# Two layers of attention and MLP on one core: the rows' preparation for the seven-product MLP laid out anew, and the last block's h kept on chip

## The chip, the cores and the metric

The kernel runs on one core of one Trainium2 chip, in one launch. The metric is the device time in microseconds. Three runs of the kernel before gave 3548.34, 3548.96 and 3552.73 us; their median, 3548.96, is the time before.

## The reference

Two layers, with the same weights in both: x is 2048 x 640, wqkv 640 x 1920, wo 640 x 640, w1 640 x 1536, w2 1536 x 640, all fp32, 32 heads of 20 columns.

```python
x = x + _A_ref(_layernorm(x), A_wqkv, A_wo)            # attention and its output product
x = x + _B_ref(_layernorm(x), B_w1, B_b1, B_w2, B_b2)  # the MLP
# and the same two lines once more

def _B_ref(x, w1, b1, w2, b2):
    h = jnp.einsum("bsd,df->bsf", x, w1) + b1
    r = jnp.where(h > 0, h, 0)
    h = r * r
    return jnp.einsum("bsf,fd->bsd", h, w2) + b2
```

## The kernel before

**Numbers.** Each fp32 operand is split into a high part in fp32r (a cast, on ScalarE) and a low part (the rest, a subtraction, on VectorE by split_to and into, on POOL for some). A product is the sum of three: hi x hi, hi x lo, lo x hi (THREE).

**Heads.** At the end of attention, add_heads goes over four blocks of 512 rows, 0 to 3. For each of a block's four row tiles and each half of its columns it runs a chain of matmuls (L510), adds x (L1441), and calls between: 32 such points in all. At these points the first block's rows are made ready for the MLP (BESIDE_HEADS), and pieces of w_1 of 512 KB are loaded (weights_at: 20 of 24; the other four go to steps of the first block).

**A block's rows** (class Forms): four row tiles are loaded, their means and variances taken (stats, L315 on VectorE, two small operations on POOL), normalised and turned in 32 x 32 squares (turned: L348, L353 on VectorE), written to d_t and fetched back turned (fetch). Then POOL forms sums and differences (sums, third, fourth, all L342) and each operand is split: B11, B22, T1, T2, T3, T4, the fifth part of the columns (plain) and its difference (diff, giving xd). ScalarE's part of a split is L458, VectorE's L459; T3 and T4 have their low part on POOL. B21 is split last, by late(), since it shares its tile. Tile pairs 0 and 1 (rows 0 and 2, rows 1 and 3) go one after the other, so T4(1) is the last split but one. PLACES says at which step each of these stands.

**First product** (class Up). 1536 columns of h are six units of a block. One unit is a Winograd form of a 2 x 2 product, seven products in place of eight: 54 matmuls of 128 x 256 (L1461). Their order on TensorE: A11 (6), the fourth sum S4 of the unit before (9), S2 (6), S1 (6), A22 (6, and 3 on xd), S3 (9), A12 (9). VectorE adds between PSUM banks: L1499 after S2 (S3 goes on in that bank, so it waits for it), L1507, L1508 and L1509 after S3 (L1508 frees the bank that S4 takes), L1522 in the unit's tail. ScalarE applies relu (L1488) and squares (L1511, L1524), POOL forms two sums of h (L1527, L342) for the second product, and SP stores h (d_h) and a sum (d_h1). A unit calls side() seven times, after each product; so a block has 42 steps, and at step n the next block does PLACES[n], the block after that PLACES[n - 42]. At the end of a block, late() splits B21 of the next.

**Second product** (class Down): eight pairs of row tiles (un 0 to 7), seven products too, in a group of four (grp 0, L1616) and one of three (grp 1), three pairs of h columns each. h comes back by DMA (fetch, three to five steps ahead), is split by parts (L327 on ScalarE, L328 on VectorE, after a subtraction L1595 or L1603; make, two steps ahead). The first two un are interleaved, group by group. During the last block of the first product, steps 27, 29, 33 fetch the first h, 38 and 41 make the first operands, and 15 of the 28 pieces of w_2 are loaded (bring). Instructions of one engine run in the order in which the code records them; nothing reorders them later. DMAs all go through SP's queue (L78).

In the first layer the fourth block of rows does the second product plainly (blocks = 3).

Of the kernel before, what the change touches and what calls it, by code (L numbers as in the profile page):

```python
# [8 lines left out]
F32 = mybir.dt.float32  # L9
# [28 lines left out]
LAST_PREP = 22  # L38


@with_exitstack
def tile_layers(
# [320 lines left out]
    class Forms:  # L363
# [4 lines left out]
            -4: [("stats", 0)],  # L368
            -3: [("stats", 2)],
            0: [("load", 1), ("load", 3)],  # L370
            2: [("turned", 0)],
            8: [("fetch", 0)],
            9: [("turned", 2)],
            10: [("stats", 1)],
            12: [("stats", 3)],
            15: [("fetch", 2)],
            16: [("turned", 1)],
            19: [("turned", 3)],
            22: [("fetch", 1)],
            23: [("sums", 0), ("split", B11, 0)],  # L380
            24: [("third", 0), ("split", B22, 0)],
            25: [("plain", 0)],
            26: [("split", T1_, 0), ("fetch", 3)],
            27: [("split", T2_, 0)],
            28: [("fourth", 0)],
            30: [("split", T3_, 0)],
            31: [("split", T4_, 0)],
            32: [("diff", 0), ("sums", 1), ("split", B11, 1)],
            33: [("third", 1), ("split", B22, 1)],
            34: [("plain", 1)],  # L390
            35: [("split", T1_, 1)],
            37: [("split", T2_, 1), ("fourth", 1)],
            38: [("split", T3_, 1)],
            40: [("split", T4_, 1)],
            41: [("diff", 1)],
# [889 lines left out]
    def attention(first, x_src, first_rows):  # L1285
# [27 lines left out]
        def begin(i):  # L1313

            t, u = divmod(i, NKT)
            g, qb = divmod(t, NQB)
            if u == 3:
                q_t.pop(t - 1, None)
            if u == 1:
                if t + 2 < NBLK and t + 2 not in q_t:  # L1320
                    load_q(t + 2)
            if u % 4 == 1 and qb == 0:
                k_t.pop((g - 1, u // 4), None)
                for h in (0, 1, 2, 3) if g else (1, 2):
# [12 lines left out]
            if (t, u) in loads:  # L1337
                loads[t, u]()
            if t == NBLK - 1 and u == 12:
                first_rows.extend(row_tile(x_src, i) for i in range(4))  # L1340
            if i in split:
                split.pop(i)()
# [83 lines left out]
    def add_heads(qb, x_src, x_mid, xs, side):  # L1426

        ot = ready.pop(qb)
        for i in range(4):
            if qb + 1 < NQB:  # L1430
                xs.append(row_tile(x_src, qb * 4 + 4 + i))
# [12 lines left out]

    class Up:
# [36 lines left out]
        def unit(self, qb, j, x, whole, free):  # L1482
# [5 lines left out]
            relu = lambda out, src, f: nc.scalar.activation(  # L1488
                out, src, AF.Relu, bias=b1_t[:, f : f + 1]
            )  # L1490
# [15 lines left out]
            r = slot([P, 2, 4, P], F32, "r")  # L1506
            add(u0, bank[1], u0)  # L1507
            add(r[:, 1, 1::2, :], rc(bank[2]), rc(u0))  # L1508
            add(r[:, 0, 1::2, :], rc(bank[3]), rc(u0))  # L1509
            relu(r[:, :, 1::2, :], r[:, :, 1::2, :], j + NP)  # L1510
            nc.scalar.activation(r[:, :, 1::2, :], r[:, :, 1::2, :], AF.Square)  # L1511
            side()
            self.chain(bank[0], j, A12, x, True, (0, last[:, :, 0]))
            relu(r[:, 0, 0::2, :], rc(bank[0]), j)
# [5 lines left out]
            def tail():  # L1520
                self.chain(bank[2], j, S4, x, True, (0, last[:, :, 1]))
                add(r[:, 1, 0::2, :], rc(bank[2]), rc(u1))  # L1522
                relu(r[:, 1, 0::2, :], r[:, 1, 0::2, :], j)
                nc.scalar.activation(r[:, :, 0::2, :], r[:, :, 0::2, :], AF.Square)  # L1524
                s = u0.rearrange("p (u c) -> p u c", u=2)
                if whole:
# [11 lines left out]
                self.held.append(store)  # L1538
# [4 lines left out]
    class Down:  # L1543
# [4 lines left out]
        def __init__(self, blocks, x_mid, x_dst):  # L1548
            self.x_mid, self.x_dst, self.blocks = x_mid, x_dst, blocks
            self.steps = [  # L1550
                (un, grp, j) for grp in (0, 1) for j in range(NP // 2) for un in range(2)
            ]
            self.steps += [
                (un, grp, j)
                for un in range(2, 2 * NQB)
# [3 lines left out]
            self.uses = [(n, un, j) for n, (un, grp, j) in enumerate(self.steps) if grp != 1]  # L1559
# [3 lines left out]
        def fetch(self):  # L1563
# [8 lines left out]
            if qb < self.blocks:  # L1572
                s = self.s[un, j] = xtile("s")[:, : 4 * P].rearrange("p (f i c) -> p f i c", f=2, i=2)
                dma(nc.sync, s[:, 0], d_h1[qb, 2 * j : 2 * j + 2, :, u].rearrange("i p c -> p i c"))

# [42 lines left out]
        def run(self, side):  # L1618

            last_j = NP // 2 - 1  # L1620
            for n, (un, grp, j) in enumerate(self.steps):
# [12 lines left out]
                if grp and un and j == (0 if grp == 1 and un > 1 else 1):  # L1634
# [3 lines left out]
                while self.uses and self.uses[0][0] <= n + (  # L1638
                    3 if n < NP or self.uses[0][1] == 2 * NQB - 1 and self.blocks < NQB else 5
# [95 lines left out]
    def layer(first, x_a, x_m, x_e, front_0, ahead):  # L1735
# [36 lines left out]
        def between():  # L1772
            side()
            n = beside[0]
            made[0].do(Forms.BESIDE_HEADS, n)
            made[1].do(Forms.PLACES, {29: -9, 30: -4, 31: -3}.get(n))
            more(weights_at.get(n, 0))
            beside[0] += 1

        for qb in range(NQB):  # L1780
            add_heads(qb, x_a, x_m, xs, between)
            if qb > 1:
                all_steps()
        made[0].y.clear()
# [6 lines left out]
        def bring(n):  # L1791
            for _ in range(n):
# [4 lines left out]
        lead = {27: down.fetch, 29: down.fetch, 31: lambda: down.rows(0), 33: down.fetch,  # L1797
                38: down.make, 41: down.make}
        for qb in range(NQB):
            for n in range(7 * NP):  # L1800
                def step(n=n, qb=qb):
                    if qb + 1 < NQB:
                        made[qb + 1].do(Forms.PLACES, n)
                        if qb + 2 < NQB:
                            made[qb + 2].do(Forms.PLACES, n - 7 * NP)
                        if n % 3 == 1:
                            more(1)
                    else:
                        bring(int(n % 7 in (1, 4) or n % 14 == 6))
                        lead.get(n, lambda: None)()  # L1810
                steps.append(step)
            x = made[qb].res
            for j in range(NP):
                up.unit(qb, j, x, qb < blocks, qb == NQB - 1)
            all_steps()
            made[qb].res = None
            if qb + 1 < NQB:
                del x[B21]
                made[qb + 1].late()
# [3 lines left out]
        down.rows(1)  # L1823
# [85 lines left out]
```

## Time and profile before

| what | value |
|---|---|
| median of three runs | 3548.96 us |
| the profiled execution | 3550.9 us, its span 3548.8 us |
| TensorE matmul busy | 3503.0 us, 99% of the span |
| VectorE, ScalarE, POOL busy | 2776.4, 2833.4, 965.2 us |
| mean granted clock of TensorE | 0.997 |
| first product, first layer | 1444.55 to 1623.74 us |
| first product, second layer | 3213.91 to 3389.36 us |

The span is what the profiler saw on the core; the execution's own time has some 2 us more around it. The timeline gives start, duration, engine, line, operation, tiles and the count of like instructions in a row; in brackets stands how long the engine was idle before, and what released it.

### The profile page before, as it was taken

Reading aid. Unit: us, or ns where it says so; the run is one execution under the profiler, and the core shown is the slowest. Engines: PE = TensorE matmul, PEld = TensorE weight load, DVE = VectorE, ACT = ScalarE, POOL = GpSimd, SP = SyncE. Lnnn points to the kernel's source line nnn. Section 1 sums busy time; section 2 is a strip of 40 time slices with the busy share of each in tenths; the row PEclk is TensorE's granted clock in tenths of the full one; section 3 lists DMA queues with packets and bytes.
Section 4 is the critical chain, followed back from the end, with each engine's and each line's share of the span. In section 5 each row is a group of like instructions: output and inputs, shape, how many; then the busy total and the mean of one; then the engine's idle time right before and its main releaser. Section 6 shows DMA issues by size and latency. Waiting matters only on the chain. (4 is left out here: it accounts for less than half of the span.)

```text
span 3548.8 us, 74211 instructions
## 1 busy us (share of the span) xinstructions
PE 3503.0 (99%) x26404; PEld 2161.2 (61%) x26404; DVE 2776.4 (78%) x5512; ACT 2833.4 (80%) x5026; POOL 965.2 (27%) x1189
## 2 busy tenths in 40 slices
PE   9999999999999999899999999999999999999999
PEld 8998333333333336899989973333333333368999
DVE  8999888888888882666869988888888888726567
ACT  5889999999999994354348899999999999944533
POOL 4430354444321211440143201212112121214400
PEclk9999999999999999999999999999999999999999
DMA  7765444444322137758656652222232121377584
GB/s 258 231 209 184 144 137 145 122 132 135 120 69 61 52 104 256 246 182 305 240 192 226 197 170 69 79 74 61 69 85 57 43 60 52 107 274 244 196 293 146
DMA packets 335041, 534.46 MB, mean 151 GB/s; under 512 B 75604, under 2 KB 154964, under 8 KB 334672
## 3 DMA queue, kind: packets, MB, share of 16 engines
q1 hardware_dynamic: 334144, 528.02, 46.7%
q8 instruction: 209, 3.42, 0.4%
q10 hardware_dynamic: 528, 1.70, 0.1%
q14 instruction: 160, 1.31, 0.1%
HBM read 339.01 MB, written 190.55 MB: 149 GB/s over the span
## 5 line engine op out<-in xcount | busy, mean ns | idle before, releaser
L939 ACT ACTIVATE e<-banks 128x512 f32<-128x512 f32 (+1 forms) x3416 | 2035.2, 692 | 55.9 <-PE banks L929 20.7
L846 DVE TENSOR_REDUCE mx<-banks 128x1 f32<-128x512 f32 x2560 | 1620.4, 684 | 321.4 <-PE banks L835 269.9
L944 PE MATMUL banks<-e,vg 128*32 128x512 f32 x8192 | 1093.4, 605 | 2.1 <-ACT e L939 2.0
L835 PE MATMUL banks<-k,q 60*128 60x512 f32 x3360 | 1058.7, 410 | 0.0
L929 PE MATMUL banks<-q,k 62*128 62x512 f32 x4096 | 1049.8, 441 | 1.3 <-ACT v L606 0.6
L929 PEld LDWEIGHTS banks<-q,k 62*128 62x128 f32 x4096 | 515.0, 184 | 748.7 <-ACT e L939 440.9
L835 PEld LDWEIGHTS banks<-k,q 60*128 60x128 f32 x3360 | 567.7, 185 | 195.1 <-ACT e L939 63.7
L875 DVE CUSTOM_DVE_ANT_0 rl<-banks,rl 128x512 f32<-128x512 f32 x736 | 476.9, 688 | 31.0 <-PE banks L835 6.8
L868 ACT ACTIVATE rl<-banks 128x512 f32<-128x512 f32 x736 | 399.7, 602 | 57.0 <-PE banks L835 46.4
L944 PEld LDWEIGHTS banks<-e,vg 128*32 128x32 f32 x8192 | 162.2, 108 | 352.9 <-issue 269.0
L1461 PE MATMUL banks<-xf,w 128*128 128x256 f32 x2448 | 315.3, 288 | 26.7 <-DVE r L1508 10.4
L542 PE MATMUL banks<-xnT,wqk 64*128 64x512 f32 x1080 | 326.5, 392 | 0.0
L530 PE MATMUL banks<-xnT,wqk 64*128 64x512 f32 x1080 | 325.7, 393 | 0.0
L1461 PEld LDWEIGHTS banks<-xf,w 128*128 128x128 f32 x2448 | 303.1, 194 | 36.0 <-DVE r L1508 14.2
L988 POOL TENSOR_TENSOR few<-few,minus_t 128x16 f32<-128x16 f32 x62 | 179.9, 2901 | 232.1 <-DMA few<-d_s 231.9
L339 POOL CAST mr<-nt 128x32 fp32r<-128x32 f32 x64 | 13.4, 210 | 755.6 <-DVE nt L901 755.6
L999 POOL TENSOR_TENSOR o<-o 128x512 f32<-128x512 f32 x62 | 79.5, 1283 | 502.2 <-DMA o<-d_r 276.8
L835 PE MATMUL banks<-kd,q 60*128 60x512 f32 x736 | 209.9, 398 | 0.8 <-ACT rl L868 0.6
L542 PEld LDWEIGHTS banks<-xnT,wqk 64*128 64x128 f32 x1080 | 201.2, 187 | 8.6
L530 PEld LDWEIGHTS banks<-xnT,wqk 64*128 64x128 f32 x1080 | 199.3, 186 | 9.1 <-issue 1.7
L530 PE MATMUL banks<-wv,xnT 64*128 64x320 f32 x960 | 193.5, 308 | 0.0
L542 PE MATMUL banks<-wv,xnT 64*128 64x320 f32 x960 | 190.4, 306 | 0.0
(149 smaller groups left out, 3530.8 us busy)
## 6 DMA issues: line engine op xcount, KB each, us to landing
q<-d_qk SPq DMA_DIRECT2D x876, 80.0 KB
d_qk<-ev SPq DMA_DIRECT2D x80, 512.0 KB
k<-d_qk SPq DMA_DIRECT2D x444, 80.0 KB
x<-d_x SPq DMA_DIRECT2D x96, 320.0 KB
w<-d_w SPq DMA_DIRECT2D x60, 480.0 KB
w<-d_w SPq DMA_DIRECT2D x48, 512.0 KB
d_h<-r SPq DMA_DIRECT2D x48, 512.0 KB
r<-d_h SPq DMA_DIRECT2D x48, 512.0 KB
```

Of the source, the lines that this page charges most:

```text
L530: top = nc.tensor.matmul(dst, a[:64], b[:64], start=start, stop=last)
L542: low = nc.tensor.matmul(dst, a, b, start=False, stop=last, skip_group_check=True)
L835: nc.tensor.matmul(dst, q_t[t][b : b + 60, p, sub * P : (sub + 1) * P], k_t[t // NQB, c][b : b + 60, p, :], start=True, stop=True,)
L846: nc.vector.tensor_reduce(maxima(t)[:, 2 * p + par, sub, c : c + 1], dst, axis=AX.X, op=ALU.max)
L868: nc.scalar.activation(r, dst, AF.Relu)
L875: nc.vector.tensor_tensor_reduce(out=r[par], in0=dst, in1=r[par], scale=1.0, scalar=LEAST, op0=ALU.add, op1=ALU.max, accum_out=maxima(t)[: ...
L929: nc.tensor.matmul(dst, k_t[t // NQB, kt // 4][b : b + 62, p, (kt % 4) * P : (kt % 4 + 1) * P], q_t[t][b : b + 62, p, :], start=True, stop ...
L939: nc.scalar.activation(dst, src, AF.Exp, scale=SCALE)
L944: nc.tensor.matmul(acc[32 * h : 32 * h + 32, :], v_t[t // NQB, kt // 8][:, kt % 8, 32 * h : 32 * h + 32], es[p][:, par, :], start=(kt == 0 ...
L988: nc.gpsimd.tensor_tensor(few, few, minus_t, op=ALU.pow)
L999: nc.gpsimd.tensor_mul(o[:, 0, :], o[:, 0, :], o[:, 1, :])
L1461: nc.tensor.matmul(dst, w, v, start=n == 0 and not more, stop=n == len(todo) - 1, skip_group_check=more,)
```

## The change

Line numbers from 39 on go up by two, and by 16 to 42 in Up and Down (L1499 becomes L1498, L1507 to L1509 become L1523 to L1525, L1522 becomes L1546, L1595 becomes L1637).

- The heads are added in the order of blocks 1, 0, 2, 3 (HEADS), the first product goes over the blocks 1, 2, 3, 0 (UPS); the second goes from 0 up as before. The ring of PSUM tiles is set to bank 7 ahead of the heads.
- PLACES is another table: stats, fetches, sums and splits stand at other steps. late() stands at step 2 of its own block.
- Beside the heads one piece of w_1 is loaded at every odd point below 28, 14 in all; the other ten at every third step of the first block.
- The last block, block 0, keeps its h: relu and square write to six arena tiles and POOL's sums to six other tiles, which Down's first two un read. Its 24 stores and fetches a layer fall away. Relu, square and POOL's two operations there are done for each half apart. Down's operands are first made at steps 36 and 40, its rows loaded at 30, w_2 brought 22 pieces deep, and un 0 goes through both groups before un 1.

The core of the diff (of the table one line, "..." marks what is left out):

```diff
+HEADS = (1, 0, 2, 3)
+UPS = (1, 2, 3, 0)
...
-            40: [("split", T4_, 1)],
-            41: [("diff", 1)],
+            40: [("split", T3_, 1), ("fourth", 1)],
+            41: [("split", T4_, 1), ("diff", 1)],
...
-        def unit(self, qb, j, x, whole, free):
+        def unit(self, qb, j, x, whole, free, keep=None):
...
-            r = slot([P, 2, 4, P], F32, "r")
+            if keep is None:
+                r = slot([P, 2, 4, P], F32, "r")
+                of = [r[:, u] for u in range(2)]
+                pair = [r[:, :, i::2, :] for i in range(2)]
+            else:
+                of, sums = keep
+                pair = None
...
+                elif whole:
+                    for z, s in zip(of, sums):
+                        nc.gpsimd.tensor_tensor(s, z[:, 2, :], z[:, 3, :], op=ALU.add)
+                        pool_lo(z[:, 2, :], z[:, 0, :], z[:, 2, :])
...
-                self.held.append(store)
+                if pair:
+                    self.held.append(store)
...
+        def keep(self, j):
+            i = j % 2
+            for un in range(2):
+                if i == 0:
+                    self.raw[un, j // 2] = slot([P, 2, 4, P], F32, "r")
+                    self.s[un, j // 2] = xtile("s")[:, : 4 * P].rearrange(
+                        "p (f i c) -> p f i c", f=2, i=2
+                    )
+            return (
+                [self.raw[un, j // 2][:, i] for un in range(2)],
+                [self.s[un, j // 2][:, 0, i] for un in range(2)],
+            )
...
-        weights_at = {g: 1 for g in [*range(2, 8), *range(9, 15), *range(17, 23), 25, 27]}
+        ps_all.n = 7
...
-            more(weights_at.get(n, 0))
+            made[UPS[0]].do(Forms.BESIDE_HEADS, n)
+            made[UPS[1]].do(Forms.PLACES, {29: -9, 30: -3, 31: -1}.get(n))
+            more(n % 2 if n < 28 else 0)
...
-        lead = {27: down.fetch, 29: down.fetch, 31: lambda: down.rows(0), 33: down.fetch,
-                38: down.make, 41: down.make}
+        lead = {30: lambda: down.rows(0), 36: down.make, 40: down.make}
...
+                    if n == 2 and m:
+                        made[UPS[m]].late()
+                    if final:
+                        bring(int(n < 7 or n % 7 in (1, 3, 5)))
```

How the order of instructions moves, at three places.

ScalarE at the border of the first two blocks of the first layer, from the copy of u0 in the last unit (L1494, L1493) on; xf tiles are operands of the next block, t and y what they are split from (t the sums, y the turned rows). Before:

```order
L1494 COPY us_17134<-banks 128x256
L458 CAST xf_17014<-t_17090 128x2x128
L1488 ACTIVATE r_17104<-r_17104,b_t 128x2x128
L1524 ACTIVATE r_17104<-r_17104 128x4x128
L458 CAST xf_17033<-t_17090 128x2x128
L458 CAST xf_17066<-y_16919 128x2x128
L1488 ACTIVATE r_17208<-r_17208,b_t 128x4x128
L1511 ACTIVATE r_17208<-r_17208 128x4x128
L458 CAST xf_17075<-t_17090 128x2x128
```

and now:

```order
L1493 COPY us_17129<-banks 128x256
L1515 ACTIVATE r_17101<-r_17101,b_t 128x2x128
L1521 ACTIVATE r_17101<-r_17101 128x4x128
L460 CAST xf_17012<-t_17137 128x2x128
L460 CAST xf_17027<-t_17137 128x2x128
L1527 ACTIVATE r_17198<-r_17198,b_t 128x4x128
L1521 ACTIVATE r_17198<-r_17198 128x4x128
L460 CAST xf_17066<-y_16911 128x2x128
L1515 ACTIVATE r_17198<-banks,b_t 128x2x128
L460 CAST xf_17075<-t_17137 128x2x128
```

The cast of T3 (xf_17066) stood ahead of the last unit's relu and square and now stands behind them; T4's (xf_17075) has one more operation ahead of it.

POOL at the same place, from the last sum of the unit before on; the last rows are the low parts of T3 (into xf_17066) and T4 (into xf_17075) and, between t and y, "fourth". Before:

```order
L342 TENSOR_TENSOR r_17104<-r_17104 128x2x128
L342 TENSOR_TENSOR t_17090<-y_16885,t_17090 128x256
L342 TENSOR_TENSOR xf_17066<-y_16919,xf_17066 128x2x128
L318 TENSOR_TENSOR mv_17177<-mv_17177,eps_t 128x1
L319 TENSOR_TENSOR mv_17177<-mv_17177,half_t 128x1
L318 TENSOR_TENSOR mv_17193<-mv_17193,eps_t 128x1
L319 TENSOR_TENSOR mv_17193<-mv_17193,half_t 128x1
L342 TENSOR_TENSOR xf_17075<-t_17090,xf_17075 128x2x128
```

and now:

```order
L344 TENSOR_TENSOR r_17101<-r_17101 128x2x128
L320 TENSOR_TENSOR mv_17183<-mv_17183,eps_t 128x1
L321 TENSOR_TENSOR mv_17183<-mv_17183,half_t 128x1
L344 TENSOR_TENSOR xf_17066<-y_16911,xf_17066 128x2x128
L344 TENSOR_TENSOR t_17137<-y_16871,t_17137 128x256
L344 TENSOR_TENSOR xf_17075<-t_17137,xf_17075 128x2x128
```

"fourth" came ahead of T3's low part and now stands behind it; the statistics of one row tile (mv) are gone from this stretch.

VectorE at the last unit of the last block of the first layer; hb and ha are the first operands of the second product. Before:

```order
L1499 TENSOR_TENSOR us_18712<-banks,us_18712 128x256
L1595 TENSOR_TENSOR s_18624<-s_18624,r_18622 128x256
L328 TENSOR_TENSOR hb_18748<-r_18622,hb_18748 128x512
L328 TENSOR_TENSOR ha_18751<-s_18624,ha_18751 128x512
L1507 TENSOR_TENSOR us_18712<-banks,us_18712 128x256
L1508 TENSOR_TENSOR r_18774<-banks,us_18712 128x2x128
```

and now:

```order
L1637 TENSOR_TENSOR s_18308<-s_18308,r_18307 128x256
L330 TENSOR_TENSOR hb_18745<-r_18307,hb_18745 128x512
L330 TENSOR_TENSOR ha_18748<-s_18308,ha_18748 128x512
L1498 TENSOR_TENSOR us_18718<-banks,us_18718 128x256
L1523 TENSOR_TENSOR us_18718<-banks,us_18718 128x256
L1524 TENSOR_TENSOR r_18635<-banks,us_18718 128x2x128
```

The three operations of the operands stood behind the add L1499 and now stand ahead of it.

More of the change, by code (lines that the diff above doesn't have):

```diff
@@ L1339, in begin @@
             if t == NBLK - 1 and u == 12:
[L1340 removed]
+                first_rows.extend(row_tile(x_src, 4 * HEADS[0] + i) for i in range(4))
             if i in split:
@@ L1521, in tail @@
                 self.chain(bank[2], j, S4, x, True, (0, last[:, :, 1]))
[L1522 to L1526, printed above, removed]
+                add(of[1][:, 0::2, :], rc(bank[2]), rc(u1))
+                relu(1, 0)
+                square(pair[0] if pair else of[1])
+                if whole and pair:
+                    s = u0.rearrange("p (u c) -> p u c", u=2)
                     nc.gpsimd.tensor_tensor(s, r[:, :, 2, :], r[:, :, 3, :], op=ALU.add)
                     pool_lo(r[:, :, 2, :], r[:, :, 0, :], r[:, :, 2, :])
+                elif whole:
+                    for z, s in zip(of, sums):
+                        nc.gpsimd.tensor_tensor(s, z[:, 2, :], z[:, 3, :], op=ALU.add)
+                        pool_lo(z[:, 2, :], z[:, 0, :], z[:, 2, :])
                 if free:
@@ L1796, in layer, with step @@
         up = Up(side)
-        lead = {27: down.fetch, 29: down.fetch, 31: lambda: down.rows(0), 33: down.fetch,
-                38: down.make, 41: down.make}
-        for qb in range(NQB):
+        lead = {30: lambda: down.rows(0), 36: down.make, 40: down.make}
+        for m, qb in enumerate(UPS):
+            final = m == NQB - 1
             for n in range(7 * NP):
[L1801 to L1809, printed above, removed]
-                        lead.get(n, lambda: None)()
+                def step(n=n, m=m, final=final):
+                    if n == 2 and m:
+                        made[UPS[m]].late()
+                    if final:
+                        bring(int(n < 7 or n % 7 in (1, 3, 5)))
+                        lead.get(n, lambda: None)()
+                        return
+                    made[UPS[m + 1]].do(Forms.PLACES, n)
+                    if m + 2 < NQB:
+                        made[UPS[m + 2]].do(Forms.PLACES, n - 7 * NP)
+                    if n % 3 == 1:
+                        more(1)
                 steps.append(step)
             x = made[qb].res
+            if m:
+                del made[UPS[m - 1]].res[B21]
+                made[UPS[m - 1]].res = None
             for j in range(NP):
-                up.unit(qb, j, x, qb < blocks, qb == NQB - 1)
+                up.unit(qb, j, x, final or qb < blocks, final, down.keep(j) if final else None)
             all_steps()
[L1816 to L1819, printed above, removed]
+        made[UPS[-1]].res = None
         del x
```

89 lines of the change are left out of this document (49 added, 40 removed).

## The prediction

> **What bounds the kernel now.** I read the busy times on the page first, then the waits of TensorE, then TensorE's timeline through both MLPs, and last the granted clock in the stretches where it stalls.
>
> ```profile
> PE 3503.0 (99%) x26404; PEld 2161.2 (61%) x26404; DVE 2776.4 (78%) x5512; ACT 2833.4 (80%) x5026; POOL 965.2 (27%) x1189
> ```
>
> The rows of the waits of TensorE give the line that waits, what it waits for, us in total, times, the longest:
>
> ```profile
> PE banks L1461 <- DVE r L1508: 10.4, 11, 1.6
> PE banks L1461 <- DVE us L1499: 8.9, 14, 1.4
> PE banks L1616 <- ACT hb L327: 6.9, 2, 5.2
> ```
>
> TensorE is the bound: 3503.0 of a span of 3548.8 us. The change neither adds nor drops a matmul, so it can only win back lost time, and the waits put nearly all of that on the first product (L1461) and the start of the second (L1616). The timeline of TensorE in the first layer gives places (start, us, count, idle before in brackets):
>
> ```profile
> 1444.55 0.87 PE L1461 MATMUL banks<-xf,w 128*128 128x256 f32 x6
> 1448.48 0.39 PE L1461 MATMUL banks<-xf,w 128*128 128x256 f32 x1 [3.06 <-ACT xf L458]
> 1450.53 3.99 PE L1461 MATMUL banks<-xf,w 128*128 128x256 f32 x17 [1.66 <-DVE xf L459]
> ...
> 1464.09 0.52 PE L1461 MATMUL banks<-xd,w 128*128 128x256 f32 x3
> ...
> 1477.05 0.52 PE L1461 MATMUL banks<-xd,w 128*128 128x256 f32 x3
> ...
> 1492.73 3.13 PE L1461 MATMUL banks<-xf,w 128*128 128x256 f32 x24 [0.81 <-DVE us L1499]
> 1497.48 3.72 PE L1461 MATMUL banks<-xf,w 128*128 128x256 f32 x27 [1.62 <-DVE r L1508]
> ...
> 1508.07 0.52 PE L1461 MATMUL banks<-xd,w 128*128 128x256 f32 x3
> ...
> 1514.55 0.52 PE L1461 MATMUL banks<-xd,w 128*128 128x256 f32 x3
> ```
>
> The three xd matmuls mark each unit once. An undisturbed unit lasts 1514.55 - 1508.07 = 6.48 us, 0.12 a matmul. From these rows: the start should reach its second marker after 9.36 us of matmuls (24 up to the first marker, 54 more), at 1453.91, and reaches it at 1464.09: 10.2 us lost. Four units around the border of the first two blocks take 31.02 us in place of 25.92: 5.1 lost. The second layer and the second product:
>
> ```profile
> 1636.14 0.56 PE L1616 MATMUL banks<-w,hb 128*128 128x320 f32 x2 [1.68 <-ACT hb L327]
> ...
> 3213.91 0.87 PE L1461 MATMUL banks<-xf,w 128*128 128x256 f32 x6
> 3229.29 0.52 PE L1461 MATMUL banks<-xd,w 128*128 128x256 f32 x3
> 3405.32 2.44 PE L1616 MATMUL banks<-w,hb 128*128 128x320 f32 x6 [5.23 <-ACT hb L327]
> ```
>
> The second layer loses 3229.29 - 3213.91 - 9.36 = 6.0 us at its start.
>
> ```profile
> 1373.00:1444.00 71.00, 71.00 (x483) 70.34 (x480) 31.77 (x60) 4.38 (x12) 7.42 (x14) 1.00 0.97 342
> 1450.00:1460.00 10.00, 8.48 (x38) 8.19 (x39) 7.59 (x19) 1.35 (x5) 3.77 (x8) 0.50 0.78 285
> 1495.00:1500.00 5.00, 3.38 (x29) 3.18 (x28) 2.65 (x9) 2.18 (x6) 3.47 (x8) 1.00 0.74 262
> 1636.00:1641.00 5.00, 4.33 (x17) 4.07 (x18) 2.19 (x5) 1.33 (x4) 0.00 (x0) 0.66 1.04 400
> ```
>
> The last three columns are granted clock, DMA share, GB/s. The DMA engines are full (0.97) before the first product, and the clock falls to 0.50 after the 3.06 + 1.66 us of stall and to 0.66 around 1636, but stays 1.00 through the stall of 1.62.
>
> **The change, part by part.** Sums are against the profiled execution, 3550.9 us (span 3548.8); the median of the runs is 3548.96, so a sum is moved down by 1.9 at the end.
>
> A, the start of the first product. The transfer that ends last there is the fourth transposed row tile:
>
> ```profile
> w<-d_w SPq DMA_DIRECT2D x48, 512.0 KB
> 1439.30 3.17 SPq L78 DMA_DIRECT2D y<-d_t  x4
> 1446.40 0.72 POOL L342 TENSOR_TENSOR t<-y,y 128x256 f32<-128x256 f32 x1 [7.44 <-DMA y<-d_t]
> ```
>
> It was issued from 1439.30 on, and POOL, which builds the sums from it, waited 7.44 us for it. By the table of loads, 18 pieces of w_1 were issued before that fetch and 11 are now: 7 x 0.524 MB at the 342 GB/s of the window above are 10.7 us of DMA time that no longer stand ahead. That is as much as the whole lost 10.2, so what remains is set by the next thing. PSUM tiles for the heads now begin one bank later (n=7), so that the first unit's A11 takes a bank that the last head has just filled; it waits for the last add of the heads, which on VectorE stands behind stats of the next block, whose rows are loaded only two adds before. I have no row of that wait: it is at least one stats (a BN_STATS pair near 0.9, below) and at most some 4.5 us, an estimate: a load that is issued two adds earlier and takes as long as POOL waited here, 7.44, less the 3 us or so that two column halves of the heads last. Nearer the lower, since the queue is shorter: 1.3. A gives 10.2 - 1.3 = 8.9 and 6.0 - 1.3 = 4.7: -13.6 (between -8 and -15).
>
> B, the start of the second product. The 144 matmuls of its first two column pairs should need 144 x 1.76/12 = 21.1 us. The rows, of the last unit and of the second product in both layers:
>
> ```profile
> 1618.80 0.42 DVE L1499 TENSOR_TENSOR us<-banks,us 128x256 f32<-128x256 f32 x1 [0.35 <-PE banks L1461]
> 1620.34 3.56 PE L1461 MATMUL banks<-xf,w 128*128 128x256 f32 x27
> 1620.80 0.68 DVE L328 TENSOR_TENSOR ha<-s,ha 128x512 fp32r<-128x512 f32 x1
> 1623.74 1.04 PE L1616 MATMUL banks<-w,hb 128*128 128x320 f32 x6
> 1649.85 1.04 PE L1616 MATMUL banks<-w,hc 128*128 128x320 f32 x6
> 3386.13 1.22 DVE L328 TENSOR_TENSOR ha<-s,ha 128x512 fp32r<-128x512 f32 x1
> 3389.36 1.04 PE L1616 MATMUL banks<-w,hb 128*128 128x320 f32 x6
> 3392.01 1.92 PE L1616 MATMUL banks<-w,hb 128*128 128x320 f32 x12
> 3393.77 1.92 PE L1616 MATMUL banks<-w,ha 128*128 128x320 f32 x12
> 3418.16 1.04 PE L1616 MATMUL banks<-w,hc 128*128 128x320 f32 x6
> ```
>
> 1.76 is 3393.77 - 3392.01. In the second layer 3418.16 - 3389.36 = 28.8, 7.7 too many, of which 5.23 are the wait for an h read back. In the first layer 1649.85 - 1623.74 = 26.1, 5.0 too many, with 1.68 in one wait and half clock behind it. With h kept on chip neither wait exists: -5.0 and -7.7, and the second layer's last unit no longer loses the 0.5 or so that a split's 1.22 (the row of 3386.13) is over the 0.68 of the first layer's. What is late next: the first h operands are made at step 36, not 38, and on VectorE their lo parts now stand ahead of L1498 (before: L1499) of the last unit. The last of them ended at 1620.80 + 0.68 = 1621.48; with 0.42 for the add the third sum can begin at 1621.9, where it began at 1620.34: 1.6 us, and up to 2.0 with the 1.22 that this line takes in the second layer, each 1.8. B: -5.0 - 8.2 + 3.6 = -9.6 (between -5 and -12). The 24 DMAs fewer in each layer, and w_2 brought 22 pieces deep rather than 15, lie on queues that nobody there waits for once h is kept; the 24 more, shorter POOL adds are behind the same unit's relu and hold nobody.
>
> C, the borders of blocks, three in each layer. Rows of the last unit of the first block:
>
> ```profile
> 1493.88 0.77 DVE L459 TENSOR_TENSOR xf<-t,xf 128x256 fp32r<-128x256 f32 x1 [1.21 <-ACT xf L458]
> 1494.57 0.87 DVE L315 BATCH_NORM_STATS2 bst<-x 128x6 f32<-128x320 f32 x2
> 1497.34 0.41 DVE L1509 TENSOR_TENSOR r<-banks,us 128x256 f32<-128x256 f32 x1
> 1498.55 0.63 ACT L1511 ACTIVATE r<-r 128x512 f32<-128x512 f32 x1
> 1499.08 0.39 ACT L458 CAST xf<-t 128x256 fp32r<-128x256 f32 x1
> 1499.55 0.73 POOL L342 TENSOR_TENSOR xf<-t,xf 128x256 fp32r<-128x256 f32 x1 [1.37 <-ACT xf L458]
> ```
>
> Before, the split of T4 was the one thing left behind this unit's square: hi at 1499.08, lo on POOL until 1500.28, just when the next block's A22 (21 matmuls after 1497.48, 1500.0) wants it. Now T3's hi is behind the square too, and on POOL T3's lo, then "fourth", then after another cast T4's lo. From 1499.08: 0.39 + 0.08 to POOL, 0.73 (T3 lo), 0.75 (fourth, an operation of the same size), 0.45 (T4 hi), 0.75 (T4 lo): 1502.2, so A22 stalls by 2.1 where it stalled 0.2. Behind it on VectorE: the lo of xd, one stats, the tail add and the first add of the new block stand in that order, so the third sum waits 0.5; B21's split, moved from the border to step 2, ends after A12 wants it, 0.4; and B21's lo and the turned tile together put the fourth sum back by 0.9. Against that, stats of the second row tile no longer stand ahead of L1508 (0.87 + 0.2, for one more lo of some 0.6: 0.45 off the 1.62) and T1's lo no longer ahead of L1499 (0.3 off the 0.81). Net 1.9 + 0.5 + 0.4 + 0.9 - 0.75 = +2.95 at each of the first two borders. At the third no stats and no turned tile are in the way: +2.0. Twice 7.9: +15.8 (between 0, if T3 and T4 hide, and +20).
>
> D, the clock. A stall of 2.1 lies between 1.62, after which the clock held, and 1.68 + 0.53 (the two waits around 1636, as the timeline has them), after which it fell. If it falls, some 3.3 us of work run at half rate and cost 1.7. Six borders, a chance of a third: +3.
>
> The Trainium skill ("TensorE: Matmul & The Clock Gate", Part 1: The HAM clock gate) says that the array halves its clock after an idle window of some 3.4 us, windows that run freely. By that a stall of 2.1 would never be a whole idle window and D would be 0; the rows above, with a halved clock behind stalls of 2.2 spread over a window, speak for a lower point.
>
> Sum: -13.6 - 9.6 + 15.8 + 3 = -4.4, 3546.5 for a profiled execution, **3544.6** as a median.
>
> **The rivals.** R1, the borders cost nothing. If POOL takes T3 and "fourth" earlier than I think, or TensorE reaches A22 later because S4 waits on VectorE anyway, C and D are 0 and A and B stand: -23.2, 3525.8. For it: 1.62 us of stall ahead of the same matmuls give slack. Against: that stall and the square end on the same add (1497.34), so the chain keeps its length from there. R2, the clock falls at each border and stays down for two windows, as it did for the 10 us of 1450 to 1460 behind two stalls. Each border then costs 2 x 1.7; six are 20 in place of 3: -4.4 + 17 = +12.6, 3561.6. It decides where stalls within one window pass 2.2, that is, where the A22 stall of 2.1 and the 0.5 at the third sum, 1.1 us of matmuls later, fall into one window. For it: the closeness of 2.1 to 2.2. Against: the clock was 1.00 over the present border. By the skill's rule of a whole idle window R2 could not happen. R3, the kept h brings nothing, because the operands' splits on ScalarE and VectorE are as late as the fetch was: B is 0, -4.4 + 9.6 = +5.2, 3554.2. Against: ACT waits for DMA at L327 here, and the added stall is a VectorE one.
>
> **How the numbers follow.** No change, to what this measurement can tell, is within 0.2%, 7.1 us. The forecast has 0.52, its own range 3535 to 3553 from the bounds of A, B and C together; it crosses -7.1 in a third of that: 0.16 faster, 0.34 the same, 0.02 slower. R1 0.26, all faster. R2 0.17, of it 0.15 slower, 0.02 the same. R3 0.05, the same by 0.04, slower by 0.01. Faster 0.42, the same 0.40, slower 0.18. The range reaches to R1 and R2 and leaves about 0.1 beyond each: 3525 to 3561.
>
> **What would show it.** A: the second xd marker at about 11 us after the first matmul (now 19.5 and 15.4), granted clock 1.00 there. B: no wait of L1616 for a DMA behind hb, one wait of 1.6 to 2.0 on VectorE's us at the last unit. C: at each border one wait of about 2 us for the lo on POOL, and 0.4 to 0.9 behind it; the stall of 1.62 smaller. D: the clock over each border. I am wrong if the borders have no new wait (then R1), if the clock is near 0.5 over the new block's first unit (R2), or if the start still waits for the transposed tile.

## The result and the profile after

The changed kernel takes 3569.40 us (median of four runs, 3566.06 to 3571.27) against 3549.54 before (four runs): a ratio of 1.0054, with an interval of 1.0036 to 1.0071. It is slower by 20 us, where 3544.6 was forecast and 3561 was the end of the range.

The busy times of the profiled execution (3570.83 us, span 3569.1), and the waits of TensorE that belong to the MLP:

```profile
PE 3511.4 (98%) x26404; PEld 2167.9 (61%) x26404; DVE 2787.7 (78%) x5512; ACT 2837.6 (80%) x5038; POOL 973.1 (27%) x1213
```

```profile
PE banks L1463 <- DVE r L1524: 16.3, 14, 3.9
PE banks L1463 <- issue: 8.9, 2, 5.0
PE banks L1463 <- DVE us L1498: 8.5, 11, 1.6
PE banks L1463 <- ACT xf L460: 7.1, 6, 1.2
PE banks L1463 <- DVE xf L461: 2.9, 5, 1.0
PE banks L1463 <- POOL xf L344: 2.5, 6, 0.4
```

The matmuls are as many as before, but take 8.4 us more, and the mean granted clock is 0.994 in place of 0.997: more of them ran at half clock. The wait of the second product on a fetched h (6.9 before) is gone from the list. In its place stand two waits of "issue", six on a cast and six on POOL, and L1524 (L1508 before) went from 10.4 to 16.3. TensorE's timeline in the first layer says where:

```profile
1449.18 4.61 PE L1463 MATMUL banks<-xf,w 128*128 128x256 f32 x24 [5.05 <-issue]
...
1460.11 0.52 PE L1463 MATMUL banks<-xd,w 128*128 128x256 f32 x3
...
1478.88 4.99 PE L1463 MATMUL banks<-xf,w 128*128 128x256 f32 x27 [2.42 <-DVE r L1524]
...
1491.79 3.14 PE L1463 MATMUL banks<-xf,w 128*128 128x256 f32 x24 [1.07 <-DVE us L1498]
1496.42 2.78 PE L1463 MATMUL banks<-xf,w 128*128 128x256 f32 x21 [1.49 <-DVE r L1524]
1500.39 0.38 PE L1463 MATMUL banks<-xf,w 128*128 128x256 f32 x1 [1.20 <-ACT xf L460]
1501.20 0.86 PE L1463 MATMUL banks<-xf,w 128*128 128x256 f32 x5 [0.42 <-POOL xf L344]
1501.90 0.52 PE L1463 MATMUL banks<-xd,w 128*128 128x256 f32 x3
1503.01 1.86 PE L1463 MATMUL banks<-xf,w 128*128 128x256 f32 x10 [0.59 <-DVE us L1498]
1505.83 1.94 PE L1463 MATMUL banks<-xf,w 128*128 128x256 f32 x14 [0.97 <-DVE xf L461]
1508.33 3.50 PE L1463 MATMUL banks<-xf,w 128*128 128x256 f32 x27 [0.56 <-DVE r L1524]
...
1632.76 3.65 PE L1463 MATMUL banks<-xf,w 128*128 128x256 f32 x27 [1.64 <-DVE us L1498]
1636.25 1.04 PE L1658 MATMUL banks<-w,hb 128*128 128x320 f32 x6
...
1646.81 1.04 PE L1658 MATMUL banks<-w,hc 128*128 128x320 f32 x6
```

From top to bottom: 5.05 us before the first matmul of the first product; 2.42 in the fourth unit of the first block, where nothing stood before; in the block's last unit 1.07 and 1.49, where 0.81 and 1.62 stood before; at the border behind them the waits at A22 (1.20 and 0.42), S3 (0.59), A12 (0.97) and S4 (0.56), one behind the other; 1.64 at the last unit; and a second product that starts without a gap (72 matmuls in 10.56 us, 0.147 each).

To compare kernels I add up three losses in each profile, both layers together. *Start*: from the end of the heads to the second group of xd matmuls, less 9.36. *Blocks*: what the intervals between the 23 later groups have over 6.48 each. *Last*: from the last such group to the second product, less 3.6. Half clock is in these sums.

| kernel | start | blocks | last | median, us | ratio to before (interval) |
|---|---|---|---|---|---|
| before | 15.9 | 26.6 | 0.8 | 3549.54 | |
| changed | 12.0 | 58.3 | 4.1 | 3569.40 | 1.0054 (1.0036 to 1.0071) |
| bank | 13.6 | 54.1 | 4.1 | 3569.55 | 1.0049 (1.0034 to 1.0064) |
| bank, stats later | 10.0 | 55.2 | 4.1 | 3566.86 | 1.0042 (1.0028 to 1.0056) |
| w_1 as before | 24.7 | 48.8 | 4.1 | 3572.15 | 1.0056 (1.0041 to 1.0071) |
| fetches as before | 12.6 | 49.3 | 4.1 | 3563.32 | 1.0033 (1.0022 to 1.0044) |
| T3, fourth earlier | 15.7 | 45.9 | 4.1 | 3558.07 | 1.0017 (1.0007 to 1.0027) |
| table of before | 12.5 | 27.2 | 4.1 | 3539.43 | 0.9965 (0.9952 to 0.9978) |
| that, B21 at step 2 | 13.3 | 34.5 | 4.1 | 3547.72 | 0.9989 (0.9980 to 0.9999) |
| first mended kernel | 1.5 | 32.4 | 0.4 | 3530.73 | 0.9941 (0.9926 to 0.9956) |
| second mended kernel | 2.2 | 27.2 | 0.4 | 3524.93 | 0.9922 (0.9905 to 0.9938) |

The runs of before that stand beside the experiments have medians of 3551 to 3552 us, so the ratios are what to compare between rows. The losses are those of one execution each: the start differs by up to 4 us (12.0 to 15.7) between kernels that do the same there.

### The profile page after: what moved, and what is told of

It reads as the page before. It is cut to its first block, busy times and chain, and to the rows that moved or that the text cites. A ratio compares the mean times of both kernels' runs of the same rounds, so it can differ in the third digit from the quotient of the medians.

```text
span 3569.1 us, 74141 instructions
## 1 busy us (share of the span) xinstructions
PE 3511.4 (98%) x26404; PEld 2167.9 (61%) x26404; DVE 2787.7 (78%) x5512; ACT 2837.6 (80%) x5038; POOL 973.1 (27%) x1213
## 4 chain that ended last, share of the span: by engine, by line
PE 88%; DMA 4%; DVE 2%; issue 2%; ACT 2%; POOL 1%; SPq 1%; DVEq 0%; POOLq 0%; ACTq 0%
PE banks L946 27%; PE banks L931 18%; PE banks L837 17%; PE banks L1658 8%; PE banks L532 5%; PE banks L544 5%; PE banks L1463 4%; PE banks L512 2%; DMA y<-d_t 1%; SPq L80 1%; DVE xf L461 1%; DMA x<-d_x 1%; PE banks L527 1%; DMA d_t<-x 0%; PE banks L644 0%
## 5 line engine op out<-in xcount | busy, mean ns | idle before, releaser
L1463 PE MATMUL banks<-xf,w 128*128 128x256 f32 x2448 | 327.3, 293 | 46.5 <-DVE r L1524 16.3
L1463 PEld LDWEIGHTS banks<-xf,w 128*128 128x128 f32 x2448 | 313.4, 200 | 57.3 <-DVE r L1524 19.7
```

What stands on the lines that cost most here:

```text
L1463: nc.tensor.matmul(dst, w, v, start=n == 0 and not more, stop=n == len(todo) - 1, skip_group_check=more,)
```

## The experiments

The theory after the result: the change lost in the table, at the borders (the splits of T3 and T4 behind the last unit's relu and square) and in the first block; and the start got little because VectorE waits for rows. The rival: the DMA queues and the new order of blocks are to blame, whatever the table.

**The bank.** The waits of "issue" stand ahead of the first A11, whose operands were long there. The other engines beside it, in the timeline of the changed kernel:

```profile
1439.71 2.31 SPq L80 DMA_DIRECT2D x<-d_x  x2
...
1447.60 0.89 DVE L317 BATCH_NORM_STATS2 bst<-x 128x6 f32<-128x320 f32 x2 [1.32 <-DMA x<-d_x]
...
1448.64 0.44 DVE L1443 TENSOR_TENSOR x<-banks,x 128x320 f32<-128x320 f32 x1
```

VectorE waits for the rows of the next block but one, which were asked for at 1439.71 and are there at 1447.60; behind their stats stands the last add of the heads, which ends at 1449.08; and A11 begins at 1449.18, because that add empties the bank that it needs.

```diff
-        ps_all.n = 7
+        ps_all.n = 6
```

> The changed kernel with the ring of PSUM tiles set to 6 in place of 7 ahead of the heads, so that the last head's tile lies in bank 7 and not in bank 0. Theory (the start is lost to a bank: the first A11 waits for the very last add of the heads, 5.05 and 3.88 us): no wait ahead of A11 any more, but the add after S2 still stands on VectorE behind that last add and the stats of the next block, so a wait of about 3 us comes back at S3 of the first unit; net 4 to 7 us faster than the changed kernel. Rival (the start is bound by the transfers, whatever the bank): within 1 us of the changed kernel.

A11 did not wait, and a wait on VectorE took its place at S3:

```profile
1452.71 8.65 PE L1463 MATMUL banks<-xf,w 128*128 128x256 f32 x51 [3.48 <-DVE us L1498]
```

It is 3.48 here and 4.23 in the second layer, a little more than expected, and the clock fell behind it as it did before. Start 13.6 in place of 12.0, and the time the same: the gain of 4 to 7 us did not come, and by the time alone the rival would be right. The wait itself stands where the theory put it, behind the stats: the bank decides where it stands, not whether there is one.

**Bank, and stats later.** Taken out of the heads, the stats stand at steps 2 and 4 of the first block.

```diff
-            made[UPS[1]].do(Forms.PLACES, {29: -9, 30: -3, 31: -1}.get(n))
+            made[UPS[1]].do(Forms.PLACES, {29: -9}.get(n))
...
+                    if not m:
+                        made[UPS[1]].do(Forms.PLACES, {2: -3, 4: -1}.get(n))
```

> The same, and the stats of the next block's first two row tiles taken out of the heads, to steps 2 and 4 of the first block. Theory (bank and stats together are the whole loss of the start): first product starts without a wait over 1.5 us, 9 to 12 us faster than the changed kernel. Rival (transfers): no more than the run with the bank alone.

```profile
1453.82 5.01 PE L1463 MATMUL banks<-xf,w 128*128 128x256 f32 x27 [2.75 <-DVE r L1524]
```

It missed too, with some 3 us in place of 9 to 12: the wait moved on to S4, 2.75 and 3.76 us, where L1524 stands behind the stats. At step 2 VectorE still waits for the rows (0.27 us in the first layer, 1.26 in the second), then 0.93 for POOL's part of these stats, since the first turned tile (step 3) now comes right behind them; the turning and the second stats stand ahead of L1524 too. Half of the theory holds (VectorE in its order, behind a load); that two or four steps are enough did not.

**The pieces of w_1.** 20 beside the heads and 4 in the first block, as before.

```diff
-            more(n % 2 if n < 28 else 0)
+            more(weights_at.get(n, 0))
```

> The changed kernel with 20 pieces of w_1 beside the heads as before, 4 in the first block in place of 10. Theory (the waits of 2.42 and 3.88 us at S4 in the first block come from the pieces moved into it, which stand ahead of the transposed rows in the DMA queues): those two waits fall under 1 us, 8 to 10 us there; against it the start gets up to 3 us worse in each layer; net 3 to 8 us faster. Rival (they come from the fetches put two steps later by the table): both waits stay over 2 us, time the same or slower.

```profile
1455.18 5.46 PE L1463 MATMUL banks<-xf,w 128*128 128x256 f32 x24 [11.17 <-issue]
```

The waits in the fourth unit went (blocks 9.5 us better), and the start lost 12.7: 11.17 us now pass before A11. VectorE's last split and its stats, with the add that empties the bank behind them, in the same profile:

```profile
1447.03 2.23 DVE L461 TENSOR_TENSOR xf<-y,xf 128x256 fp32r<-128x256 f32 x3 [2.15 <-ACT xf L460]
...
1452.87 0.42 DVE L461 TENSOR_TENSOR xd<-t,xd 128x128 fp32r<-128x128 f32 x1 [1.27 <-POOL xf L344]
...
1454.64 0.44 DVE L1443 TENSOR_TENSOR x<-banks,x 128x320 f32<-128x320 f32 x1
```

The fourth transposed tile is late again, the splits wait for it, and the add stands behind them: the end of VectorE's row comes at 1455.08. The theory is right on what the pieces do in the block, and far off on what they cost beside the heads. Term A's first half is right, then: seven pieces fewer make that tile early enough. The add behind the stats then took what was won.

**The table.**

```diff
-        PLACES = { ... }   # the table of the change
+        PLACES = { ... }   # the table of before
...
-                    if n == 2 and m:
-                        made[UPS[m]].late()
+                made[UPS[m + 1]].late()   # at the end of a block
```

> The changed kernel with the table of before and late() at the border as before; order of blocks, kept h, loads and bank as changed. Theory (the table costs the borders: 48.8 us lost there in the profile after, 26.9 before): 18 to 28 us faster than the changed kernel, so 10 or so faster than before. Rival (the borders are lost to the other order of blocks or to the DMA queue): within 5 us of the changed kernel.

The blocks lose 27.2 us in place of 58.3, as in the kernel before, and the time is 0.9965 of before: 31 us faster than the change, 12 faster than before. Without the changed table nothing is lost in the blocks: the order of blocks and the kept h cost nothing there, and the moved pieces of w_1 cost there only together with the table, as the run before this one and the next one show. The next three runs take the table apart.

**The fetches.** Only fetch(0) and fetch(2) go back.

```diff
-            10: [("fetch", 0)],
-            17: [("fetch", 2)],
+            8: [("fetch", 0)],
+            15: [("fetch", 2)],
```

> The changed kernel with the first two fetches of turned rows back at steps 8 and 15 (changed: 10 and 17), the rest of the table as changed. The wait at S4 in the first block (2.42 and 3.88 us, 9 us with the clock) was gone both with the table of before and with fewer pieces of w_1 there. Theory (the fetch two steps later and the pieces ahead of it together are what is late): both waits under 1 us, 7 to 9 us faster than the changed kernel. Rival (the sums on POOL, put two steps earlier by the table, hold up the splits): waits as they are, no change.

```profile
1477.95 3.50 PE L1463 MATMUL banks<-xf,w 128*128 128x256 f32 x27 [0.49 <-DVE r L1524]
```

0.49 in place of 2.42 (0.61 in place of 3.88): blocks 9.0 us better, time 7 (the seven runs of this kernel spread from 3558.72 to 3570.07, and the profile is of the shortest). In the stretches by window, the changed kernel and the one before, the DMA queues (the share next to last) say why two steps were too many:

```profile
1470.00:1480.00 10.00, 7.58 (x63) 7.38 (x63) 5.70 (x11) 4.47 (x12) 4.14 (x6) 1.00 1.06 342
```

```profile
1470.00:1480.00 10.00, 10.00 (x86) 10.00 (x85) 8.10 (x14) 4.40 (x11) 4.51 (x6) 1.00 0.67 220
```

With the pieces of w_1 moved into the first block the queues are full there (1.06, against 0.67), and a fetch that is issued later comes too late for the splits that VectorE does ahead of L1524.

**T3 and "fourth" earlier.** The chain as forecast, on ScalarE and POOL of the changed kernel:

```profile
1497.48 0.63 ACT L1521 ACTIVATE r<-r 128x512 f32<-128x512 f32 x1
1498.02 0.39 ACT L460 CAST xf<-y 128x256 fp32r<-128x256 f32 x1
1498.49 0.73 POOL L344 TENSOR_TENSOR xf<-y,xf 128x256 fp32r<-128x256 f32 x1 [1.98 <-ACT xf L460]
1499.18 0.72 POOL L344 TENSOR_TENSOR t<-y,t 128x256 f32<-128x256 f32 x1
1499.94 0.40 ACT L460 CAST xf<-t 128x256 fp32r<-128x256 f32 x1 [1.15 <-POOL t L344]
...
1500.42 0.72 POOL L344 TENSOR_TENSOR xf<-t,xf 128x256 fp32r<-128x256 f32 x1 [0.52 <-ACT xf L460]
```

Square, T3's cast, its low part, fourth, T4's cast, its low part: each begins when the one ahead ends, and TensorE takes up T4 at 1500.39 and its low part at 1501.20.

```diff
-            38: [("split", T2_, 1)],
-            40: [("split", T3_, 1), ("fourth", 1)],
-            41: [("split", T4_, 1), ("diff", 1)],
+            38: [("split", T2_, 1), ("fourth", 1), ("split", T3_, 1)],
+            40: [("split", T4_, 1)],
+            41: [("diff", 1)],
```

> The changed kernel with three entries at the end of the table moved: fourth(1) and T3(1) at step 38, T4(1) at 40, diff(1) at 41, so that they stand ahead of the last unit's relu and square on ScalarE as before. Theory (the chain square, T3, fourth, T4 through ScalarE and POOL is what A22 of the next block waits for): the waits of 1.20 and 0.42 at all six borders go, and the wait at S3 behind them shrinks: 9 to 14 us faster than the changed kernel. Rival (the splits are late on POOL for want of the sums, whatever ScalarE does): 0 to 3 us.

At the first border nothing is left of the wait at A22, and S3 waits as long as it did:

```profile
1499.52 3.73 PE L1463 MATMUL banks<-xf,w 128*128 128x256 f32 x27 [1.50 <-DVE r L1524]
1503.09 0.52 PE L1463 MATMUL banks<-xd,w 128*128 128x256 f32 x3
1504.19 1.86 PE L1463 MATMUL banks<-xf,w 128*128 128x256 f32 x10 [0.59 <-DVE us L1498]
```

12.4 us come back in the blocks, 2.1 a border, and the ratio falls by 0.0037, 13 us. Confirmed, but for the S3 wait, which is VectorE's own (stats and the low part of xd) and did not shrink.

**B21 at step 2**, with the table of before. It is the run "table of before" with late() at step 2, as changed.

> The kernel with the table of before, but with the split of B21 at step 2 as changed (in the run before with that table it stood at the border). Theory (the move costs 0.4 at A12 and some 0.5 at S4, since B21's low part then stands ahead of the turned tile on VectorE): 3 to 6 us slower than the run with the table of before alone. Rival (it is hidden, and takes the ScalarE and VectorE work out of the border): the same or up to 4 us faster.

Blocks 34.5 in place of 27.2, and 8 us slower: more than expected, nearly all of it in the first unit of a new block (2.3 over, where 0.54 was). VectorE's two low parts of B21, first in this run, then in the run with the table of before:

```profile
1499.95 1.63 DVE L461 TENSOR_TENSOR xf<-y,xf 128x256 fp32r<-128x256 f32 x2 [1.21 <-ACT xf L460]
```

```profile
1497.68 0.76 DVE L461 TENSOR_TENSOR xf<-y,xf 128x256 fp32r<-128x256 f32 x2
```

0.76 where POOL is idle, 1.63 where the same two operations meet POOL's sums of h. And they wait 1.21 for a cast that has gone behind the unit's last square. A12 then waits for them (0.97 at each such border) and S4 for the turned tile behind them (0.56).

**A mended kernel.** Table of before, ring at 6, the first block's stats at steps 5, 13 and 17, turned tiles 0 and 2 at 9 and 12, fetch(0) at 11, the first operands of the second product at 38 and 41.

```diff
-        lead = {30: lambda: down.rows(0), 36: down.make, 40: down.make}
+        lead = {30: lambda: down.rows(0), 38: down.make, 41: down.make}
```

> The table of before, B21 at the border, the PSUM ring one bank earlier, in the first block the stats and turned tiles some 5 to 7 steps later so that VectorE doesn't wait for their rows, and the first operands of the second product made at steps 38 and 41 as before. Theory (what is left of the start, 6.7 and 6.2 us, is VectorE waiting for those rows, and the last unit's 2.05 us is the order of the operands): starts lose under 3 us each, the last unit under 0.5; 9 to 13 us faster than the run with the table of before alone, about 3528 where before is 3550. Rival (the start is bound by the transfers): 3 to 4 us faster, from the last unit alone.

The second marker of the first layer, and the one wait ahead of it:

```profile
1448.64 0.86 PE L1463 MATMUL banks<-xf,w 128*128 128x256 f32 x5 [0.56 <-POOL xf L344]
...
1456.14 0.52 PE L1463 MATMUL banks<-xd,w 128*128 128x256 f32 x3
```

The starts lose 1.2 and 0.3 us, the last units 0.2 each: both halves confirmed, and with them that the start was lost to VectorE's order, with its adds behind stats whose rows were late, and not to the transfers whatever the order. How much each of the moved steps is worth, this run does not separate. 5 us are given back in the first block, by the wait that the changed kernel had there: the rows are turned and fetched later, VectorE's splits wait for them, and L1524 stands behind the splits.

```profile
1472.72 2.09 DVE L461 TENSOR_TENSOR xf<-y,xf 128x256 fp32r<-128x256 f32 x3 [1.81 <-ACT xf L460]
...
1475.66 3.50 PE L1463 MATMUL banks<-xf,w 128*128 128x256 f32 x27 [2.62 <-DVE r L1524]
```

In the second layer there is less of this (1.28), and 1.39 of waiting for a piece of w_1. The ratio is 0.9941, 21 us faster than before and 9 faster than the table of before alone.

**Stats out of the last unit.**

```diff
-                    } if not m else {}, n)
-                    if m or n not in (2, 8, 9, 10, 12):
+                    } if not m else {2: [("stats", 0), ("stats", 2)], 5: [("turned", 0)]}, n)
+                    if n not in ((2,) if m else (2, 8, 9, 10, 12)):
...
-                        made[UPS[m + 2]].do(Forms.PLACES, n - 7 * NP)
+                        if n == 33:
+                            made[UPS[m + 2]].do(Forms.PLACES, -9)
```

> The best kernel so far (table of before, later stats in the first block, PSUM ring one earlier, operands at 38 and 41), with the stats of the first two row tiles of the next but one block taken from steps 38 and 39 of a block's last unit to step 2 of the next block, and the first turned tile from step 2 to 5. Theory (the wait of 1.62 at S4 of a block's last unit, at four of the six borders, is VectorE doing those two stats, 2.1 us, ahead of L1524): the four waits fall under 0.7; with what step 2 costs, 3 to 6 us faster than that kernel, 0.993 of before. Rival (the casts of T1 and T2 that stand there too hold L1524 up): the waits stay over 1.2, time the same within 2 us.

The first border has only this left:

```profile
1489.08 6.48 PE L1463 MATMUL banks<-xf,w 128*128 128x256 f32 x51 [0.58 <-DVE us L1498]
1496.22 6.38 PE L1463 MATMUL banks<-xf,w 128*128 128x256 f32 x51 [0.30 <-DVE us L1498]
```

The wait of 1.6 at S4 is gone at all four borders. At the two second ones a wait of 1.89 at S3 of the last unit has come up instead of 0.80: VectorE has a split ahead of that add (L1498) which waits 1.01 for its cast, and on ScalarE the cast stands behind a copy (L1493) that waits 1.14 for TensorE. The ratio is 0.9922 (0.9905 to 0.9938), 27 us faster than before and the best of the runs.

## Why the prediction was wrong

- **A, the start, was the largest error of one term**, 9.7 of the 24.7 us between -4.4 and the measured 20.3. It was to bring -13.6 and brought 12.0 - 15.9 = -3.9. The step that failed is the price of the wait that had no row: between one stats and 4.5 us, taken at 1.3 because the queue was to be shorter. It was 5.05 and 3.88 us, and the half clock behind it, which A had at nothing, took 1.6 and 1.5 more. The load took 7.9 us from its issue to the stats, although fewer pieces of w_1 were asked for ahead of it than before; that is no shorter than the 7.44 that the upper end, 4.5, was made from. That end was the value to take (the two waits have a mean of 4.47). What the step left out is that the wait isn't tied to the bank: S3's add stands behind the same stats, so that the wait is there in any case, as the run with another bank shows. The sign that A named came true for another reason: the second xd marker stands 10.9 us after the first matmul in both layers, as forecast, but the loss had gone ahead of the first matmul, and that sign counts from there.
- **B, the second product, was right.** No wait on h (-12.7 us by the two stretches, 5.0 and 7.7) and 1.64 at each last unit, forecast 1.6 to 2.0: 4.1 - 0.8 = +3.3, in all -9.4 against -9.6.
- **C and D, the borders, had the right mechanism, and C was too small.** T3, fourth and T4 one behind the other, waits at A22, S3, A12 and S4 in that order; 1.62, 0.59, 0.97 and 0.56 at the first border where 2.1, 0.5, 0.4 and 0.9 were forecast. By unit, the six borders cost 22.7 us more than before, forecast 15.8 + 3. With the clock at 1.00, each of the first two borders of a layer costs 4.2 more (the two intervals around it are 4.63 and 3.29 over 6.48 at the second border of the run with w_1 as before, and 3.16 and 0.55 in the kernel before), where C had 2.95. The runs put 12.4 of the 22.7 on the chain of T4, which C had at 1.9 for each of six, and 7.3 on B21, which it had at 0.4 at A12 and, together with the turned tile, at 0.9 at S4, without POOL's sums beside it. The 0.75 that C took off again, for work no longer ahead of the adds, came only in part: 1.07 and 1.49 for 0.81 and 1.62 at the first border, 0.47 and 1.50 for 0.80 and 1.61 at the second. Some 3 us of the 22.7 no run takes apart.
- **What no step had** is the wait in the fourth unit of the first block: 4.2 and 5.4 us with the clock, 9 in all. I had costed the moved pieces of w_1 where they had been and not where they went, and the later fetches not at all. A moved DMA has two ends. With the chain of T4 and B21 this makes 28.7 of the 31.1 us that the table costs in the blocks (58.3 against 27.2).
- **The sum.** -3.9 - 9.4 + 31.7 = +18.4, against 20.3 between the spans. Most of the other 1.9 lie where the second layer's attention begins: matmul by matmul against the profile before, the changed kernel falls 2.2 us further behind there, with a wait of 0.75 for a transfer (d_qk, at 1814.77) and the clock at 0.50 from 1814.59 to 1818.00. The run with the table of before has such a wait too (0.94 at 1800.35), the run with the fetches as before has none, so it isn't the table's; whether the change has any part in it stays open.
- **The rivals.** R1 did not happen, and neither did R3, since B came as forecast. R2 came near on the clock and was wrong on its price. Over the six borders the granted clock was 1.00, 0.64, 0.81, 0.89, 0.80 and 0.89 in stretches of 9 to 19 us, so that it fell at five of them, where D had counted two. But TensorE waits less for the others while it is slow: at the second border the two intervals are 4.62 and 4.39 with the clock down, against 4.63 and 3.29 above, 1.1 us more where R2 had 3.4. Waiting, not the clock, makes most of the loss at the borders. None of the three had a wait in the first block.

## What to carry to other kernels

Price a moved transfer at its new place, by the DMA share of that window, and ask there who waits for what is queued behind it. A term without a row, between a small and a large bound, belongs at the bound that comes from the same kind of event (a load in a full queue), not at the one that suits the sum. And on engines that work in order, a bank or a step moved by itself only moves the wait: what has to move is the operation that waits for the load.

## What the runs showed of the hardware

The granted clock of the changed kernel in two windows:

```profile
1478.88:1483.71 4.83, 4.83 (x27) 4.83 (x28) 1.79 (x5) 3.90 (x9) 1.73 (x4) 0.65 1.08 289
1551.40:1561.00 9.60, 8.98 (x50) 8.69 (x51) 6.86 (x13) 4.48 (x10) 2.46 (x5) 0.64 0.26 102
```

One stall of 2.42 us is enough for the clock to fall: the 2.42 cost 4.2 in the interval of the unit, 1.7 of it at half rate, as D had priced a fall. The second window follows three stalls at the second border, the longest of them 1.20. The Trainium skill ("TensorE: Matmul & The Clock Gate", Part 1: The HAM clock gate) speaks of at least one idle window of some 3.4 us; at these two places no stall was that long, so the measurement decides: less is enough.

The traces say more. Within each profile the falls of the clock lie whole multiples of 3.41 us apart, and a fall goes with the idle time between two such times rather than with the length of one stall. The stretch ahead of the fall in the fourth unit and the half-clock one behind it, in the changed kernel, and the stretch around the 1.62 us stall in the kernel before, where the clock held:

```profile
1476.67:1480.08 3.41, 1.20 (x10) 1.20 (x11) 2.46 (x5) 0.85 (x2) 3.11 (x5) 1.00 1.08 355
1480.08:1483.49 3.41, 3.41 (x19) 3.41 (x18) 1.51 (x4) 2.82 (x8) 0.73 (x1) 0.50 1.05 295
```

```profile
1494.25:1497.66 3.41, 1.79 (x15) 1.59 (x14) 3.31 (x10) 0.00 (x0) 3.18 (x8) 1.00 0.46 178
```

TensorE was idle for 2.21 us of the first and for 1.62 of the last. Over all eleven profiles, each such stretch with 1.82 us or more without a matmul had half clock behind it; in the two products none with less than 1.37 had, and of those between only some.

A low part on VectorE that reads two tiles in SBUF took 0.38 alone and 0.81 beside POOL's additions (0.76 and 1.63 for two, above). The Trainium skill ("SBUF — State Buffer", Who interferes with whom) gives a rule for it: an operation with two inputs in SBUF and a GpSimd operation that reads SBUF hold one port pair in turn, each for its whole length. These rows agree that the two hinder each other; how long each holds the ports they don't show. It is part of the price that was missing for B21.
